# Multi-query attention with 16-wide heads: two heads share 32 rows of a query set, and two masked copies of the keys tell them apart

## The chip, the cores and the metric

The kernel runs on one core of one Trainium2 chip. The time is device microseconds of one execution; several executions are taken and the median is quoted. Two kernels are compared through runs taken in the same rounds on the same chip. A difference under 2% counts as "same".

Engine names as in the profile: PE is the tensor engine, ACT the scalar engine, DVE the vector engine, POOL the GpSimd engine, SP the queue that issues DMAs.

## The reference, cut to what matters

Two identical layers, each an attention block and a gated mixer block. Sequence 2048, model width 512, 32 heads of 16, one shared key and value head:

```python
q = (x @ wq).reshape(B, S, 32, 16).transpose(0, 2, 1, 3)
k = x @ wk                                   # one key head for all 32 query heads
v = x @ wv
p = softmax(einsum('bhqd,bkd->bhqk', q, k) * 16 ** -0.5)
o = einsum('bhqk,bkd->bhqd', p, v)           # then @ wo
# x = x + A(layernorm(x)); x = x + B(layernorm(x)); both twice
```

B is the mixer: gelu, a 2048 x 2048 mix over the sequence, and an output projection.

## The kernel before

The work of attention is 4096 *blocks*: 128 keys by 512 queries of one head, 2048 in each layer. A block is one matmul with 32 contracted rows, one exponential over 128 x 512, and one value matmul. Four heads sit at partitions 0, 32, 64 and 96 of a *query set* of 512 columns. A head has only 16 numbers per query, so 16 of each 32 rows are zeros that come out of zero-padded weights:

```python
# zero-padded query weights: 8 groups of 4 heads, each head 16 columns of weight and 16 of zero
wqv = self.wq_pad[:].rearrange("p kd hg (j r) -> p kd (hg j) r", r=32)[:, :, :, 0:DH]
c0 = rows(wqv[:, :, 0:8, :], wqn[:, :, 0:8, :], m, lq[0], 512, 1.2)                # ACT
c1 = rows(wqv[:, :, 8:32, :], wqn[:, :, 8:32, :], m, lq[1], 1536, 3.0, "pool")     # POOL
# ... cut: one query set = 4 heads x 512 columns: PE projects, DVE or ACT evicts
ins = e.matmul(self.b32(b)[:, i * n:(i + 1) * n], self.wq_pad[:, kd, g.hg + i, :],
               self.xnTA[:, g.t0 // 128:(g.t0 + n) // 128, kd, :], start=(kd == 0), stop=(kd == KD - 1))
# ... cut: the score matmul of one block
return e.matmul(self.b32(bank), self.kT[32 * j:32 * j + 32, kt * 128:(kt + 1) * 128],
                self.qs[32 * j:32 * j + 32, g.q.slot, :], tile_position=(32 * j, 0), start=True, stop=True)
```

ACT takes most blocks, two or three at a time. DVE takes the rest: it copies the scores out of PSUM with a multiply-add and runs a polynomial for the exponential, about 2.5 us a block.

This file does not write its instructions down; it *plans* them. At build time a list scheduler walks through all operations with assumed durations and latencies, decides for every engine which operation comes next, which engine evicts a bank (copies a result out of PSUM, where matmuls write), and which blocks go to DVE, and then writes out that fixed order:

```python
LAT = {"pe": 0.22, "act": 0.22, "dve": 0.14, "pool": 0.12, "sp": 0.0}   # assumed latency of a result, us
AHEAD = 1200.0   # more warm-up near the ends of a head group
WARM = 800.0     # warm-up: how many columns above 3060 per 3.41 us the planner keeps PE at
NQS = 6          # slots for query sets
# ... cut: the warm-up stream puts in a matmul on zeros whenever PE would fall below the limit
t = sc.below(f, TICK_COLS + WARM + (AHEAD if near else 0.0))
# ... cut: priority of a query set (small is early)
pr = 0.4 if g.ci == 0 and g.hg == 0 else 0.8 if g.hg < 2 else (2.2 if ... else 1.5)
```

The softmax here doesn't subtract the row's maximum and nothing guards it: scores larger than these inputs give would overflow.

Of the kernel before, what the change touches and what calls it, by code (L numbers as in the profile page):

```python
# [13 lines left out]
P = 128  # L14
# [361 lines left out]
AHEAD = 1200.0  # L376
# [3 lines left out]
WARM = 800.0  # L380
# [3 lines left out]
NQS = 6  # L384
# [9 lines left out]
def d_sb(n, rate):  # L394
    return n * rate + 0.066
# [14 lines left out]
class Group:  # L410

    __slots__ = ("layer", "ci", "hg", "nh", "t0", "n", "units", "q", "evac", "index")


class QSet:
    __slots__ = ("grp", "op", "slot", "left", "reads", "index")
# [10 lines left out]
class Kern:  # L427
    def __init__(self, nc, A_x, A_wq, A_wk, A_wv, A_wo, B_x, B_w_in, B_w_sp, B_b_sp, B_w_out, out):
# [27 lines left out]
        self.kT = sb([P, S], BF16, "kT")  # L456
        self.V = sb([P, self.NT, 128], BF16, "V")
        self.wq_pad = sb([P, KD, 8, 128], BF16, "wq_pad")
# [98 lines left out]
    def load(self, A_x, A_wq, A_wk, A_wv, A_wo, B_b_sp):  # L557
        sc = self.sc
        xs = A_x[0].rearrange("(t p) d -> p t d", p=P)
        wq_nat = self.z1s[:, 0:2048].rearrange("p (kd n) -> p kd n", kd=KD)  # L560
        wk_nat = self.z1s[:, 2048:2112].rearrange("p (kd n) -> p kd n", kd=KD)
        wv_nat = self.z1s[:, 2112:2176].rearrange("p (kd n) -> p kd n", kd=KD)
# [11 lines left out]
        def ld_q(c0, c1, eng):  # L574
            return self.dma(lambda e: e.dma_start(wq_nat[:, :, c0:c1], wq_d[:, :, c0:c1]), (), f"ldq{c0}", 1024 * (c1 - c0),
                            1.2 if eng == "act" else 5.0, eng)
# [31 lines left out]
        def vm(ap, n, prio):  # L608
            return sc.op("dve", lambda e: e.memset(ap, 0.0), d_sb(n, 0.26e-3), (), prio)

        def rows(dst, src, m, ld, n, prio, eng="act"):
            if eng == "act":
                return sc.op("act", lambda e: e.activation(dst, src, ACTF.Copy), d_act(n), [m, ld], prio)
            return sc.op("pool", lambda e: e.tensor_copy(dst, src), n * 1.0e-3 + 0.2, [m, ld], prio)
        m = vm(self.wk_rep[:], 512, 0.1)
        self.c_wk = rows(self.wk_rep[:].rearrange("p kd (g r) -> p kd g r", r=32)[:, :, :, 0:DH],
                         wk_nat[:, :, None, :].to_broadcast([P, KD, 4, DH]), m, lk, 256, 1.0)
# [3 lines left out]
        m = vm(self.wq_pad[:], 4096, 0.11)  # L621
        wqv = self.wq_pad[:].rearrange("p kd hg (j r) -> p kd (hg j) r", r=32)[:, :, :, 0:DH]
        wqn = wq_nat.rearrange("p kd (h r) -> p kd h r", r=DH)
        c0 = rows(wqv[:, :, 0:8, :], wqn[:, :, 0:8, :], m, lq[0], 512, 1.2)
        c1 = rows(wqv[:, :, 8:32, :], wqn[:, :, 8:32, :], m, lq[1], 1536, 3.0, "pool")
        self.c_wq = [c0, c0] + [c1] * 6
        m = vm(self.V[:], 2048, 0.13)
        self.z1s_free = [self.c_wk, self.c_wv, c0, c1]
# [55 lines left out]
    def layer_keys(self, layer):  # L684
        sc = self.sc
        for p in range(8):
            def build(p=p):
# [25 lines left out]
                def kcp(b):  # L713
                    return self.kT[:, p * 256:(p + 1) * 256], self.b32(b)[:, 0:256]

                def vcp(b):
# [3 lines left out]
                kc = dict(fn=lambda e, b: e.tensor_copy(*kcp(b)), dur=d_psum(256), prio=pr - 0.1, deps=kd_,  # L720
                          alts=[("act", lambda e, b: e.activation(*kcp(b), ACTF.Copy), d_act(256) + 0.1)])
                vc = dict(fn=lambda e, b: e.tensor_copy(*vcp(b)), dur=d_psum(128), prio=pr, deps=[self.c_v] + vd_,  # L722
                          alts=[("act", lambda e, b: e.activation(*vcp(b), ACTF.Copy), d_act(128) + 0.1)])
                if p < 2:
                    _, (k,) = sc.job([(kpe, 4 * d_mm(256))], [kc], evs + [self.c_wk], pr)
                    _, (v,) = sc.job([(vpe, 8 * d_mm(128))], [vc], evs + [self.c_wv], 0.9)
                else:
                    _, (k, v) = sc.job([((lambda e, b: (kpe(e, b), vpe(e, b))[1]), 4 * d_mm(256) + 8 * d_mm(128))], [kc, vc],
                                       evs + [self.c_wk, self.c_wv], pr)
                self.xnTA_ev[(layer, p)] = evs  # L730
                for t in ts:
                    self.k_op[(layer, t)] = k
# [10 lines left out]
    def layer_groups(self, layer):  # L743
        t0 = 0
        for ci, n in enumerate(self.chunks):
            nh = 512 // n
            for hg in range(0, 8, nh):
                g = Group()
                g.layer, g.ci, g.hg, g.nh, g.t0, g.n = layer, ci, hg, nh, t0, n
                g.index = len(self.groups)  # L750
                q = g.q = QSet()
                q.grp, q.op, q.left, q.reads = g, None, 4 * self.NT, []
                q.index = g.index
                q.slot = q.index % NQS
                self.qsets.append(q)
# [34 lines left out]
    def make_q(self, q, war=()):  # L790
# [4 lines left out]
        def pe(e, b, h):  # L795
            ins = None
            for i in range(g.nh):
# [961 lines left out]
```

## Time and profile before

| | before |
|---|---|
| median, 3 runs | 1837.04 us (1836.0 to 1838.01) |
| ACT, DVE, PE busy | 95%, 93%, 86% |
| first exponential starts | 18.1 us |
| from the last exponential of layer 1 to the first of layer 2 | 869.2 to 907.5 us |
| last exponential ends, execution ends | 1781.0, 1834.8 us |

The page's first lines, busy time by engine:

```profile
span 1834.8 us, 30175 instructions
## 1 busy us (share of the span) xinstructions
PE 1583.2 (86%) x11848; PEld 476.9 (26%) x11934; DVE 1704.0 (93%) x2917; ACT 1741.6 (95%) x1572; POOL 50.8 (3%) x90
```

The shares average over stages. The table by windows splits them: the first layer's exponentials, the first 100 us of the second layer, the rest of its exponentials, and the end. Columns: window, its length, busy us of PE, PEld, DVE, ACT and POOL, granted clock, DMA share, GB/s.

```profile
18.00:868.00 850.00, 733.07 (x5618) 213.33 (x5653) 792.70 (x1310) 844.71 (x737) 17.34 (x28) 1.00 0.16 41
907.00:1007.00 100.00, 82.59 (x611) 27.45 (x614) 87.74 (x170) 83.90 (x89) 5.76 (x12) 0.98 0.15 30
1007.00:1781.00 774.00, 670.55 (x5060) 189.22 (x5091) 728.51 (x1202) 770.49 (x668) 15.15 (x22) 1.00 0.08 23
1781.00:1835.00 54.00, 48.32 (x270) 22.79 (x273) 44.90 (x110) 19.19 (x38) 1.09 (x2) 1.00 0.31 95
```

In the first and third row ACT is busy for all but 5.3 and 3.5 us: it is the wall there, and nothing that PE or DVE saves counts unless it takes work or waiting from ACT. In the second row ACT idles 16 us; it waits for the second layer's keys, which follow the first layer's last mixer steps. In the fourth it has little to do.

The groups by form. Columns: line, engine, operation, tiles, shapes, count, then busy us and mean ns of one, then idle time before them and its releasers.

```profile
L1378 ACT ACTIVATE Pa<-ps_all 128x1536 bf16<-128x1536 f32 x716 | 1147.1, 1602 | 11.0 <-PE ps_all L1706 9.5
L1378 ACT ACTIVATE Pa<-ps_all 128x1024 bf16<-128x1024 f32 x715 | 843.3, 1179 | 1.0 <-PE ps_all L1706 0.8
...
L1562 DVE TENSOR_SCALAR E<-ps_all 128x512 f32<-128x512 f32 x516 | 351.2, 684 | 27.1 <-PE ps_all L1706 24.1
...
L1687 PE MATMUL ps_all<-zero 128*128 128x512 bf16 x846 | 269.1, 391 | 15.2 <-DVE st L1034 3.2 <-ACT z2n L1014 1.5 <-DVE gp L1133 1.5
...
L800 PE MATMUL ps_all<-xnTA,wq_pad 128*128 128x512 bf16 x192 | 54.4, 394 | 2.1 <-DVE V L722 0.9 <-DVE qs L809 0.8 <-DVE E L1562 0.2
...
L809 DVE CAST qs<-ps_all 128x512 bf16<-128x512 f32 x58 | 39.7, 684 | 4.0 <-PE ps_all L800 3.7
...
L721 ACT ACTIVATE kT<-ps_all 128x256 bf16<-128x256 f32 x16 | 6.8, 426 | 8.7 <-PE ps_all L708 5.5 <-PE ps_all L700 3.2
...
L810 ACT ACTIVATE qs<-ps_all 128x512 bf16<-128x512 f32 x6 | 3.6, 597 | 4.7 <-PE ps_all L800 4.7
```

Line 1562 counts the blocks that DVE takes: 516. Lines 809 and 810 are the 64 query evictions, line 721 the 16 key copies, line 800 the query projections (with smaller forms, 73.3 us of PE), line 1687 the warm-up matmuls.

The start, as ACT saw it; columns of the timeline are start, us, engine, line, operation, tiles, shapes, count, and in brackets the idle time before it:

```profile
12.61 0.60 ACT L678 ACTIVATE xnTA<-ps_all 128x512 bf16<-128x512 bf16 x1 [2.12 <-PE ps_all L670]
13.91 0.38 ACT L721 ACTIVATE kT<-ps_all 128x256 bf16<-128x256 f32 x1 [0.70 <-PE ps_all L700]
15.50 0.60 ACT L810 ACTIVATE qs<-ps_all 128x512 bf16<-128x512 f32 x1 [1.20 <-PE ps_all L800]
17.20 0.60 ACT L810 ACTIVATE qs<-ps_all 128x512 bf16<-128x512 f32 x1 [1.11 <-PE ps_all L800]
17.77 0.28 ACT L723 ACTIVATE V<-ps_all 128x128 bf16<-128x128 f32 x1
18.10 1.45 ACT L1378 ACTIVATE Pa<-ps_all 128x1536 bf16<-128x1536 f32 x1
```

Two query sets are evicted before the first exponential, though it needs one. Line 678 waits for PE's transpose of a tile `xn` that DVE makes in line 653. The POOL copy of the padded weights:

```profile
10.51 1.46 POOL L614 COPY wq_pad<-z1s 128x1536 bf16<-128x1536 bf16 x1
```

```profile
9.76 0.41 DVE L653 TENSOR_SCALAR xn<-X,mv,rs 128x512 bf16<-128x512 bf16 x1
...
10.76 1.37 DVE L653 TENSOR_SCALAR xn<-X,mv,rs 128x512 bf16<-128x512 bf16 x1
```

The same DVE instruction takes 0.41 us without that copy and 1.37 us while POOL copies the padded weights.

### The profile page before, as it was taken

To read this page: it belongs to the slowest core of one execution; us is meant where nothing else is said; L and a number is where in the kernel's file an instruction comes from. 1 tells how busy PE (TensorE), PEld (TensorE's weight loads), DVE (VectorE), ACT (ScalarE), POOL (GpSimd) and SP (SyncE) were. 2 spreads that over 40 slices of the span, in tenths; PEclk is the share of its full clock that TensorE was granted. 3 is DMA by queue.
4 is the path that set the end of the run, shared out by engine and by line. 5 is a ranking of instruction groups with operands and counts; after the bars stand their busy time and mean duration, and the time that the engine had idled before them with its cause. 6 is when DMAs were issued, how large, how long until landed. Compare 5 with 4: busy or idle time off the path is not lost.

```text
span 1834.8 us, 30175 instructions
## 1 busy us (share of the span) xinstructions
PE 1583.2 (86%) x11848; PEld 476.9 (26%) x11934; DVE 1704.0 (93%) x2917; ACT 1741.6 (95%) x1572; POOL 50.8 (3%) x90
## 2 busy tenths in 40 slices
PE   8888898888889889898888788887888899999898
PEld 3222222222222222232432222222222222222234
DVE  8999999999999999976879999999999999998778
ACT  7999999999999999999569999999999999999983
POOL 2000000000000000000100000000000000000000
PEclk9999999999999999999999999999999999999999
DMA  9800010000010010111120000100000100103023
GB/s 260 218 1 1 7 41 1 1 1 18 7 41 24 24 47 29 39 58 56 52 50 1 1 1 9 38 1 1 1 18 7 41 24 24 47 21 96 9 56 111
DMA packets 122965, 68.04 MB, mean 37 GB/s; under 512 B 76997, under 2 KB 119241, under 8 KB 122825
## 3 DMA queue, kind: packets, MB, share of 16 engines
q1 hardware_dynamic: 121240, 65.95, 13.3%
q8 instruction: 95, 1.56, 0.3%
q10 hardware_dynamic: 1584, 0.16, 0.1%
q14 instruction: 46, 0.37, 0.1%
HBM read 30.97 MB, written 17.83 MB: 27 GB/s over the span
## 4 chain that ended last, share of the span: by engine, by line
ACT 43%; PE 21%; issue 18%; DVE 17%; DMA 0%; POOL 0%; ACTq 0%; POOLq 0%
ACT Pa L1378 41%; PE ps_all L1120 5%; PE ps_all L1706 5%; PE ps_all L1454 3%; DVE E L1562 3%; PE ps_all L1212 2%; DVE Pd L1593 2%; DVE E L1591 1%; DVE E L1587 1%; DVE E L1589 1%; PE ps_all L1687 1%; DVE st L638 1%; DVE z2n L954 1%; PE ps_all L800 1%; DVE E L1590 1%
## 5 line engine op out<-in xcount | busy, mean ns | idle before, releaser
L1378 ACT ACTIVATE Pa<-ps_all 128x1536 bf16<-128x1536 f32 (+1 forms) x1433 | 1627.7, 1390 | 12.0 <-PE ps_all L1706 10.3
L1706 PE MATMUL ps_all<-qs,kT 32*128 32x512 bf16 x4096 | 566.2, 386 | 202.7 <-ACT Pa L1378 187.8
L1562 DVE TENSOR_SCALAR E<-ps_all 128x512 f32<-128x512 f32 x516 | 351.2, 684 | 27.1 <-PE ps_all L1706 24.1
L1706 PEld LDWEIGHTS ps_all<-qs,kT 32*128 32x128 bf16 x4096 | 139.3, 91 | 758.1 <-ACT Pa L1378 710.3
L1454 PE MATMUL ps_all<-Pa,V 128*32 128x512 bf16 x3580 | 322.8, 386 | 0.0
L1593 DVE SCALAR_TENSOR_TENSOR Pd<-E 128x1024 uint16<-128x1024 f32 x260 | 314.6, 1210 | 4.4
L1687 PE MATMUL ps_all<-zero 128*128 128x512 bf16 x846 | 269.1, 391 | 15.2 <-DVE st L1034 3.2
L1120 PE MATMUL ps_all<-wsT,z2n 128*128 128x512 bf16 x655 | 186.6, 382 | 7.1 <-issue 3.5
L1454 PE MATMUL ps_all<-Pd,V 128*32 128x512 bf16 x516 | 182.3, 385 | 0.0
L1589 DVE TENSOR_TENSOR E<-E 128x1024 f16<-128x1024 f16 x260 | 176.9, 680 | 4.9
L1591 DVE TENSOR_TENSOR E<-E 128x1024 f16<-128x1024 f16 x260 | 177.1, 681 | 4.2
L1587 DVE TENSOR_SCALAR E<-E 128x1024 f16<-128x1024 uint16 x260 | 176.6, 679 | 1.5
L1590 DVE TENSOR_SCALAR E<-E 128x1024 f16<-128x1024 f16 x260 | 107.5, 413 | 1.9
L1687 PEld LDWEIGHTS ps_all<-zero 128*128 128x128 bf16 x846 | 62.9, 98 | 150.6 <-issue 98.6
L1133 DVE TENSOR_TENSOR gp<-ps_all,gp 128x512 f16<-128x512 f32 x112 | 75.5, 684 | 24.1 <-PE ps_all L1120 23.8
L1454 PEld LDWEIGHTS ps_all<-Pa,V 128*32 128x32 bf16 x3580 | 64.5, 94 | 121.5 <-issue 118.5
L1120 PEld LDWEIGHTS ps_all<-wsT,z2n 128*128 128x128 bf16 x714 | 53.7, 97 | 99.3 <-issue 58.5
L800 PE MATMUL ps_all<-xnTA,wq_pad 128*128 128x512 bf16 (+2 forms) x384 | 73.3, 316 | 2.2 <-DVE V L722 0.9
L943 PE MATMUL ps_all<-w_in_r,xnTB 128*128 128x448 bf16 x256 | 63.5, 356 | 2.0 <-DVE E L1562 0.7
L979 PE MATMUL ps_all<-xnTB,w_in_r 128*128 128x512 bf16 (+2 forms) x336 | 62.4, 310 | 1.0 <-DVE gp L990 0.2
L1212 PE MATMUL ps_all<-E 128*128 128x512 bf16 x213 | 52.0, 380 | 4.2 <-DVE E L1197 2.0
L642 POOL TENSOR_SCALAR ve<-mv 128x2 f32<-128x2 f32 (+1 forms) x28 | 9.2, 330 | 1383.9 <-DVE mv L640 1383.7
(88 smaller groups left out, 1002.6 us busy)
## 6 DMA issues: line engine op xcount, KB each, us to landing
wsT_scratch<-gp SPq DMA_DIRECT2D x16, 512.0 KB, 3.6
wsT<-wsT_scratch SPq DMA_DIRECT2D x8, 1024.0 KB, 5.2
z1s<-z_scratch SPq DMA_DIRECT2D x16, 448.0 KB, 3.8
wsT<-wsT_scratch SPq DMA_DIRECT2D x8, 512.0 KB, 3.6
z_scratch<-z1s SPq DMA_DIRECT2D x4, 896.0 KB, 5.2
X<-in_A_x_dram SPq DMA_DIRECT2D x8, 256.0 KB, 5.5
out_dram<-X SPq DMA_DIRECT2D x16, 128.0 KB, 1.9
w_in_r<-in_B_w_in_dram SPq DMA_DIRECT2D x1, 1792.0 KB, 10.0
```

The source lines that it names most:

```text
L800: ins = e.matmul(self.b32(b)[:, i * n:(i + 1) * n], self.wq_pad[:, kd, g.hg + i, :], self.xnTA[:, g.t0 // 128:(g.t0 + n) // 128, kd, :], s ...
L1120: ins = e.matmul(self.b32(b), self.z2n[:, s, f * 128:(f + 1) * 128], w_[:, s - s0, :] if s - s0 < na or not spare else wsp[:, s - s0 - na, :],
L1378: return e.activation(k.Pa[:, base:base + n, :], k.b32(b0, n).rearrange("p (k q) -> p k q", k=n), ACTF.Exp, scale=SCALE)
L1454: ins = e.matmul(k.b32(k.pvb)[32 * j:32 * j + 32, :], k.V[:, u.kt, 32 * j:32 * j + 32], b.slot, tile_position=(0, 32 * j), start=u.first, ...
L1562: c = k.sc.op("dve", lambda e: e.tensor_scalar(k.ey[:, s, 512 * i:512 * (i + 1)], k.b32(j.bank.idx)[:, 0:512], E_LOG2, E_BIAS, op0=ALU.mul ...
L1587: o2 = sc.op("dve", lambda e: e.tensor_scalar(x, lo, E_X * 2.0 ** -16, E_X * E_A, op0=ALU.mult, op1=ALU.add), d_sb(n, 0.521e-3), self.ops ...
L1589: o3 = sc.op("dve", lambda e: e.tensor_tensor(w, x, x, ALU.mult), d_sb(n, 0.521e-3), [o2, self.wfree], pr)
L1590: o4 = sc.op("dve", lambda e: e.tensor_scalar(w, w, E_C, None, op0=ALU.add), d_sb(n, 0.26e-3), [o3], pr)
L1591: o5 = sc.op("dve", lambda e: e.tensor_tensor(w, w, x, ALU.mult), d_sb(n, 0.521e-3), [o4], pr)
L1593: o7 = sc.op("dve", lambda e: e.scalar_tensor_tensor(po.bitcast(U16), y, E_D, w, op0=ALU.add, op1=ALU.add), d_sb(n, 1.042e-3), [o5] + self ...
L1687: return e.matmul(k.b32(k.pvb if b is None else b.idx), k.zero[:], k.zero[:, None, :].to_broadcast([P, 4, P]), start=b is not None, stop=b ...
L1706: return e.matmul(self.b32(bank), self.kT[32 * j:32 * j + 32, kt * 128:(kt + 1) * 128], self.qs[32 * j:32 * j + 32, g.q.slot, :], tile_pos ...
```

## The change

The 16 zero rows are given to a second head. A query set now carries eight heads, and the plain weight needs no padding: columns 128 s to 128 s + 127 are eight whole heads. To keep the two heads of 32 rows apart there are two copies of the keys, one with the lower 16 rows of each 32 zero, one with the upper. So 64 query sets become 32 and 16 key copies become 32. Score matmuls, exponentials and value matmuls stay as they are. Two constants of the warm-up and the number of slots were set anew as well. The core of the diff, cuts marked:

```diff
-AHEAD = 1200.0
+AHEAD = 0.0
-WARM = 800.0
+WARM = 1200.0
-NQS = 6
+NQS = 4
 ... (cut)
-        self.kT = sb([P, S], BF16, "kT")
+        self.kT = sb([P, 2, S], BF16, "kT")
+        self.mask = sb([P, 2], FP32, "mask")
-        self.wq_pad = sb([P, KD, 8, 128], BF16, "wq_pad")
+        self.wq_r = sb([P, KD, D], BF16, "wq_r")
 ... (cut: the memset and the two padding copies go; wq is loaded straight into wq_r)
-                kc = dict(fn=lambda e, b: e.tensor_copy(*kcp(b)), dur=d_psum(256), prio=pr - 0.1, deps=kd_,
-                          alts=[("act", lambda e, b: e.activation(*kcp(b), ACTF.Copy), d_act(256) + 0.1)])
+                ks = [dict(fn=lambda e, b, v=v: e.tensor_scalar(*kcp(b, v), self.mask[:, v:v + 1], None, op0=ALU.mult),
+                           dur=d_psum(256), prio=pr - 0.1 + 0.2 * v, deps=kd_ + [self.c_mask[v]],
+                           alts=[("act", lambda e, b, v=v: e.activation(*kcp(b, v), ACTF.Copy, scale=self.mask[:, v:v + 1]),
+                                  d_act(256) + 0.1)]) for v in range(2)]
 ... (cut: groups come in pairs v = 0, 1 that share a query set)
-                        ins = e.matmul(self.b32(b)[:, i * n:(i + 1) * n], self.wq_pad[:, kd, g.hg + i, :],
+                        ins = e.matmul(self.b32(b)[:, i * n:(i + 1) * n], self.wq_r[:, kd, 128 * (q.s0 + i):128 * (q.s0 + i + 1)],
 ... (cut)
-        pr = 0.4 if g.ci == 0 and g.hg == 0 else 0.8 if g.hg < 2 else (2.2 if g.layer == 1 and g.ci == 0 and g.hg < NQS else 1.5)
+        pr = (0.4 if g.ci == 0 else 0.8) if q.s0 == 0 else (2.2 if g.layer == 1 and g.ci == 0 and q.s0 < NQS - 1 else 1.5)
 ... (cut)
-    return e.matmul(self.b32(bank), self.kT[32 * j:32 * j + 32, kt * 128:(kt + 1) * 128],
+    return e.matmul(self.b32(bank), self.kT[32 * j:32 * j + 32, g.v, kt * 128:(kt + 1) * 128],
```

More of the change, by code (lines that the diff above doesn't have):

```diff
@@ L410 @@
 class Group:
-    __slots__ = ("layer", "ci", "hg", "nh", "t0", "n", "units", "q", "evac", "index")
+    __slots__ = ("layer", "ci", "v", "t0", "n", "units", "q", "evac", "index")
 class QSet:
-    __slots__ = ("grp", "op", "slot", "left", "reads", "index")
+    __slots__ = ("grp", "s0", "ns", "op", "slot", "left", "reads", "index")
 class Unit:
@@ L559, in load @@
         xs = A_x[0].rearrange("(t p) d -> p t d", p=P)
-        wq_nat = self.z1s[:, 0:2048].rearrange("p (kd n) -> p kd n", kd=KD)
-        wk_nat = self.z1s[:, 2048:2112].rearrange("p (kd n) -> p kd n", kd=KD)
-        wv_nat = self.z1s[:, 2112:2176].rearrange("p (kd n) -> p kd n", kd=KD)
+        wk_nat = self.z1s[:, 0:64].rearrange("p (kd n) -> p kd n", kd=KD)
+        wv_nat = self.z1s[:, 64:128].rearrange("p (kd n) -> p kd n", kd=KD)
         def ld_x(p):
@@ L574, in ld_q @@
         def ld_q(c0, c1, eng):
-            return self.dma(lambda e: e.dma_start(wq_nat[:, :, c0:c1], wq_d[:, :, c0:c1]), (), f"ldq{c0}", 1024 * (c1 - c0),
+            return self.dma(lambda e: e.dma_start(self.wq_r[:, :, c0:c1], wq_d[:, :, c0:c1]), (), f"ldq{c0}", 1024 * (c1 - c0),
                             1.2 if eng == "act" else 5.0, eng)
@@ L607, in load, with vm @@
         self.c_mh = pm(self.mhalf[:], -0.5, 1, 0.3)
-        def vm(ap, n, prio):
-            return sc.op("dve", lambda e: e.memset(ap, 0.0), d_sb(n, 0.26e-3), (), prio)
+        def vm(ap, n, prio, val=0.0, deps=()):
+            return sc.op("dve", lambda e: e.memset(ap, val), d_sb(n, 0.26e-3), deps, prio)
         def rows(dst, src, m, ld, n, prio, eng="act"):
@@ L614, in rows @@
             return sc.op("pool", lambda e: e.tensor_copy(dst, src), n * 1.0e-3 + 0.2, [m, ld], prio)
-        m = vm(self.wk_rep[:], 512, 0.1)
-        self.c_wk = rows(self.wk_rep[:].rearrange("p kd (g r) -> p kd g r", r=32)[:, :, :, 0:DH],
-                         wk_nat[:, :, None, :].to_broadcast([P, KD, 4, DH]), m, lk, 256, 1.0)
+        m = vm(self.mask[:, 0:1], 1, 0.05)
+        for j in range(4):
+            m = vm(self.mask[32 * j:32 * j + DH, 0:1], 1, 0.05, 1.0, [m])
+        self.c_mask = [m, sc.op("dve", lambda e: e.tensor_scalar(self.mask[:, 1:2], self.mask[:, 0:1], -1.0, 1.0, op0=ALU.mult,
+                                                                 op1=ALU.add), 0.07, [m], 0.06)]
+        self.c_wk = rows(self.wk_rep[:].rearrange("p kd (g r) -> p kd g r", r=DH),
+                         wk_nat[:, :, None, :].to_broadcast([P, KD, 8, DH]), None, lk, 512, 1.0)
         m = vm(self.wv_rep[:], 512, 0.12)
@@ L620, in load @@
                          wv_nat[:, :, None, :].to_broadcast([P, KD, 4, DH]), m, lv, 256, 1.1)
-        m = vm(self.wq_pad[:], 4096, 0.11)
-        wqv = self.wq_pad[:].rearrange("p kd hg (j r) -> p kd (hg j) r", r=32)[:, :, :, 0:DH]
-        wqn = wq_nat.rearrange("p kd (h r) -> p kd h r", r=DH)
-        c0 = rows(wqv[:, :, 0:8, :], wqn[:, :, 0:8, :], m, lq[0], 512, 1.2)
-        c1 = rows(wqv[:, :, 8:32, :], wqn[:, :, 8:32, :], m, lq[1], 1536, 3.0, "pool")
-        self.c_wq = [c0, c0] + [c1] * 6
+        self.c_wq = [lq[0]] + [lq[1]] * 3
         m = vm(self.V[:], 2048, 0.13)
-        self.z1s_free = [self.c_wk, self.c_wv, c0, c1]
+        self.z1s_free = [self.c_wk, self.c_wv]
         self.c_v = pm(self.V[:].rearrange("p t (c r) -> p t c r", r=32)[:, :, :, DH], 1.0, 64, 0.8, [m])
@@ L711, in vpe, with kcp @@
                     return ins
-                def kcp(b):
-                    return self.kT[:, p * 256:(p + 1) * 256], self.b32(b)[:, 0:256]
+                def kcp(b, v):
+                    return self.kT[:, v, p * 256:(p + 1) * 256], self.b32(b)[:, 0:256]
                 def vcp(b):
@@ L724, in build @@
                 if p < 2:
-                    _, (k,) = sc.job([(kpe, 4 * d_mm(256))], [kc], evs + [self.c_wk], pr)
+                    _, k = sc.job([(kpe, 4 * d_mm(256))], ks, evs + [self.c_wk], pr)
                     _, (v,) = sc.job([(vpe, 8 * d_mm(128))], [vc], evs + [self.c_wv], 0.9)
                 else:
-                    _, (k, v) = sc.job([((lambda e, b: (kpe(e, b), vpe(e, b))[1]), 4 * d_mm(256) + 8 * d_mm(128))], [kc, vc],
-                                       evs + [self.c_wk, self.c_wv], pr)
+                    _, (k0, v, k1) = sc.job([((lambda e, b: (kpe(e, b), vpe(e, b))[1]), 4 * d_mm(256) + 8 * d_mm(128))],
+                                            [ks[0], vc, ks[1]], evs + [self.c_wk, self.c_wv], pr)
+                    k = [k0, k1]
                 self.xnTA_ev[(layer, p)] = evs
                 for t in ts:
-                    self.k_op[(layer, t)] = k
+                    self.k_op[(layer, 0, t)], self.k_op[(layer, 1, t)] = k
                     self.v_op[(layer, t)] = v
@@ L745, in layer_groups @@
         for ci, n in enumerate(self.chunks):
-            nh = 512 // n
-            for hg in range(0, 8, nh):
+            ns = 512 // n
+            for s0, v in [(s, v) for s in range(0, 4, ns) for v in range(2)]:
                 g = Group()
-                g.layer, g.ci, g.hg, g.nh, g.t0, g.n = layer, ci, hg, nh, t0, n
+                g.layer, g.ci, g.v, g.t0, g.n = layer, ci, v, t0, n
                 g.index = len(self.groups)
-                q = g.q = QSet()
-                q.grp, q.op, q.left, q.reads = g, None, 4 * self.NT, []
-                q.index = g.index
-                q.slot = q.index % NQS
-                self.qsets.append(q)
+                if v == 0:
+                    q = QSet()
+                    q.grp, q.s0, q.ns, q.op, q.left, q.reads = g, s0, ns, None, 8 * self.NT, []
+                    q.index = len(self.qsets)
+                    q.slot = q.index % NQS
+                    self.qsets.append(q)
+                g.q = q
                 g.units = []
@@ L796, in pe @@
             ins = None
-            for i in range(g.nh):
-                for kd in ((0, 1), (2, 3))[h] if g.nh == 1 else range(4):
-                    if g.nh == 1 or i // (g.nh // 2) == h:
-                        ins = e.matmul(self.b32(b)[:, i * n:(i + 1) * n], self.wq_pad[:, kd, g.hg + i, :],
+            for i in range(q.ns):
+                for kd in ((0, 1), (2, 3))[h] if q.ns == 1 else range(4):
+                    if q.ns == 1 or i // (q.ns // 2) == h:
+                        ins = e.matmul(self.b32(b)[:, i * n:(i + 1) * n], self.wq_r[:, kd, 128 * (q.s0 + i):128 * (q.s0 + i + 1)],
                                        self.xnTA[:, g.t0 // 128:(g.t0 + n) // 128, kd, :], start=(kd == 0), stop=(kd == KD - 1))
@@ L806, in make_q @@
         pairs = range(g.t0 // 256, (g.t0 + n - 1) // 256 + 1)
-        pr = 0.4 if g.ci == 0 and g.hg == 0 else 0.8 if g.hg < 2 else (2.2 if g.layer == 1 and g.ci == 0 and g.hg < NQS else 1.5)
-        pe_last, (op,) = sc.job([((lambda e, b: pe(e, b, 0)), 2 * g.nh * d_mm(n)), ((lambda e, b: pe(e, b, 1)), 2 * g.nh * d_mm(n))],
+        pr = (0.4 if g.ci == 0 else 0.8) if q.s0 == 0 else (2.2 if g.layer == 1 and g.ci == 0 and q.s0 < NQS - 1 else 1.5)
+        pe_last, (op,) = sc.job([((lambda e, b: pe(e, b, 0)), 2 * q.ns * d_mm(n)), ((lambda e, b: pe(e, b, 1)), 2 * q.ns * d_mm(n))],
                                 [dict(fn=lambda e, b: e.tensor_copy(*cp(b)), dur=d_psum(512), prio=pr, deps=list(war),
                                       alts=[("act", lambda e, b: e.activation(*cp(b), ACTF.Copy), d_act(512) + 0.1)])],
-                                [x for p in pairs for x in self.xnTA_ev[(g.layer, p)]] + self.c_wq[g.hg:g.hg + g.nh], pr)
+                                [x for p in pairs for x in self.xnTA_ev[(g.layer, p)]] + self.c_wq[q.s0:q.s0 + q.ns], pr)
         q.op = op
@@ L839, in nm @@
             if g.n == 128:
-                out = self.on[:, 0, g.hg * 64:(g.hg + 4) * 64].rearrange("p (i j d) -> p i j d", j=4, d=DH)
+                out = self.on[:, 0, :].rearrange("p (i j v d) -> p i j v d", j=4, v=2, d=DH)[:, :, :, g.v, :]
                 s0, s1 = 0, 4
             else:
-                hg = g.hg + h
-                out = self.on[:, 0:nq, hg * 64:(hg + 1) * 64].rearrange("p i (j d) -> p i j d", d=DH)
+                c = 128 * (g.q.s0 + h)
+                out = self.on[:, 0:nq, c:c + 128].rearrange("p i (j v d) -> p i j v d", j=4, v=2)[:, :, :, g.v, :]
                 s0, s1 = h * nq, (h + 1) * nq
@@ L858, in finish_group @@
         self.norms.append(m)
-        if g.hg + g.nh == 8:
+        if g.v == 1 and g.q.s0 + g.q.ns == 4:
             norms = self.norms
@@ L1287, in peek @@
             deps.append(g.q.op)
-            o = k.k_op.get((g.layer, b.unit.kt))
+            o = k.k_op.get((g.layer, g.v, b.unit.kt))
             if o is None or o.start is None:
@@ L1495, in deps @@
         g = x.unit.grp
-        return [g.q.op, k.k_op[(g.layer, x.unit.kt)]]
+        return [g.q.op, k.k_op[(g.layer, g.v, x.unit.kt)]]
     def take(self, t, js):
@@ L1535, in take @@
                 return None
-            o = k.k_op.get((layer, un.kt))
+            o = k.k_op.get((layer, un.grp.v, un.kt))
             if o is None or o.start is None or o.vis > t:
```

## The prediction

> **What bounds the kernel now.** The page gives ScalarE (ACT) 95%, VectorE (DVE) 93%, PE 86% of 1834.8 us. By 50-us windows, from 50 to about 840 us and from 1000 to about 1740 us ACT is busy 49 to 50 of every 50 us, nearly all of it the exponentials of line 1378; DVE mostly 47 to 49.5, PE 40 to 47. In the groups by form, line 1378 is busy 1627.7 us for 3580 score blocks, 0.455 us of ACT each; the other 516 blocks go through DVE's polynomial (lines 1562, 1587 to 1593: 1304 us, 2.53 us of DVE each). So ACT is the wall, and DVE relieves it at 5.6 us for 1. ACT idles about 93 us in all: the start (first exponential at 18.1 us), the change of layers (869 to about 965 us) and the closing mixer (from about 1780 us), where PE, DVE and latency lead.
>
> **What the change does.**
> 1. Query projections halve: 64 sets become 32. Line 800 costs PE 73.3 us; 36.7 us go. But warm-up matmuls (line 1687, 846, 269 us, 13 us of a window in mid-layer) are issued whenever the stream falls below a column limit and refill this; WARM up from 800 to 1200 adds more. PE stays at 85 to 90%. PE is not the wall, so this is worth almost nothing outside the start and the change of layers.
> 2. Query evictions halve: 64 of 512 columns, 58 on DVE at 0.684 us. About 20 us of DVE and 1 to 2 us of ACT go.
> 3. Key copies double, 16 more. A masked copy from PSUM should cost what a plain one does: the Trainium skill, "VectorE: DVE Perf Modes", section "Why PSUM operands drop a tier", holds fp32 PSUM operands to the 1x mode; the trace agrees, cast and multiply-add of 128x512 both take 0.68 us. 16 x 0.38 = +6 us, most on DVE.
> 4. The padded weights go: a 1.77-us DVE memset, a 0.63-us ACT copy and a 1.46-us POOL copy in the first 12 us. The first query set serves eight heads, so the second (4 matmuls, 0.4 us each) no longer goes ahead of the first scores.
> 5. Score and value matmuls and exponentials stay.
>
> **What it is worth.** Net DVE saving about 16 us. If DVE turns it into blocks, both engines stay full and the span falls by 16 x 0.455/(2.53+0.455) = 2.4 us, 5 more blocks on DVE. ACT savings, about 1 us, count nearly whole. Start: 2 us. Change of layers: one query set before the first scores, fewer evictions: 1.5 us. Clock: five windows after the start show 0.97; the skill's "TensorE: Matmul & The Clock Gate", Part 1, gives a window of about 3.4 us at half or full rate, and 0.03 x 50 us agrees with one half-rate interval. ACT loses about 0.7 us in such a window; the higher WARM may recover 2 us. Freer banks and PE in the dense mixer windows: 1 to 2 us. Sum about 11 us.
>
> **Prediction: 1826 us, 1813 to 1836; faster by over 2% 0.04, within 2% 0.94, slower by over 2% 0.02.**
>
> **What would show it.** Line 800 about 37 us; query evictions 32; key copies 32 at about 0.38 us; warm-up matmuls over 950; DVE blocks 520 to 535; ACT full mid-layer; first exponential at 15.5 to 17 us; fewer 0.97 windows.
>
> **What would make it wrong.** Extra warm-up matmuls delaying scores so that ACT waits; the chained second key copy holding banks in the change of layers (slower); a reshuffled order that lets DVE take many more blocks (faster).

## The result, and the profile after

| | before | after |
|---|---|---|
| median of 4 runs each | 1836.52 us (1835.57 to 1838.01) | 1832.13 us (1832.09 to 1835.02) |
| ratio | 1 | 0.9979 (95% interval 0.9962 to 0.9997) |
| span of the profiled run | 1834.8 us | 1830.0 us |

A ratio is the mean time of one kernel's runs over that of the other's of the same rounds, so it is not quite the ratio of the medians quoted. The change made the kernel about 4 us faster. I had forecast 11.

The lines that answer to those of before, page, windows, groups:

```profile
span 1830.0 us, 30222 instructions
## 1 busy us (share of the span) xinstructions
PE 1597.4 (87%) x11863; PEld 480.3 (26%) x11947; DVE 1697.1 (93%) x2924; ACT 1739.0 (95%) x1565; POOL 49.1 (3%) x89
```

```profile
14.00:863.00 849.00, 740.81 (x5621) 212.95 (x5654) 794.50 (x1322) 843.62 (x734) 19.87 (x30) 1.00 0.16 43
901.00:1001.00 100.00, 84.32 (x618) 27.66 (x619) 89.58 (x180) 82.42 (x84) 5.86 (x12) 0.98 0.14 30
1001.00:1775.00 774.00, 678.63 (x5071) 193.78 (x5103) 724.14 (x1192) 768.60 (x664) 13.62 (x22) 0.99 0.09 23
1775.00:1830.00 55.00, 49.75 (x276) 23.02 (x279) 44.67 (x110) 20.41 (x41) 1.10 (x2) 1.00 0.31 93
```

```profile
L1382 ACT ACTIVATE Pa<-ps_all 128x1536 bf16<-128x1536 f32 x714 | 1147.3, 1607 | 11.2 <-PE ps_all L1710 9.7
L1382 ACT ACTIVATE Pa<-ps_all 128x1024 bf16<-128x1024 f32 x716 | 846.7, 1183 | 1.6 <-PE ps_all L1710 1.5
...
L1566 DVE TENSOR_SCALAR E<-ps_all 128x512 f32<-128x512 f32 x522 | 355.1, 683 | 26.5 <-PE ps_all L1710 22.8
L1691 PE MATMUL ps_all<-zero 128*128 128x512 bf16 x1051 | 327.5, 392 | 17.4 <-ACT z1s L1014 3.2 <-DVE E L1566 2.1 <-DVE E L1593 1.8
...
L804 PE MATMUL ps_all<-xnTA,wq_r 128*128 128x512 bf16 x96 | 25.5, 381 | 1.1 <-DVE qs L813 0.5 <-DVE gp L994 0.3 <-DVE E L1566 0.3
...
L813 DVE CAST qs<-ps_all 128x512 bf16<-128x512 f32 x30 | 20.4, 679 | 0.1
...
L721 ACT ACTIVATE kT<-ps_all,mask 128x256 bf16<-128x256 f32 x16 | 7.6, 478 | 14.1 <-PE ps_all L707 11.0 <-PE ps_all L699 3.0
L719 DVE TENSOR_SCALAR kT<-ps_all,mask 128x256 bf16<-128x256 f32 x16 | 7.6, 478 | 1.7 <-ACT V L724 1.6
...
L814 ACT ACTIVATE qs<-ps_all 128x512 bf16<-128x512 f32 x2 | 1.2, 592 | 0.0
```

The counts changed as forecast: 32 evictions instead of 64, 32 key copies (at 0.478 us each and not 0.38), 1051 warm-up matmuls that more than refill PE, 522 blocks on DVE instead of 516. Yet ACT's idle time did not fall: in the second row it is 17.6 us where it was 16.1, and in the third 5.4 where it was 3.5. The start:

```profile
11.21 0.60 ACT L677 ACTIVATE xnTA<-ps_all 128x512 bf16<-128x512 bf16 x1 [0.38 <-PE ps_all L669]
12.51 0.98 ACT L721 ACTIVATE kT<-ps_all,mask 128x256 bf16<-128x256 f32 x2 [0.70 <-PE ps_all L699]
13.39 0.59 ACT L814 ACTIVATE qs<-ps_all 128x512 bf16<-128x512 f32 x1
13.87 0.28 ACT L724 ACTIVATE V<-ps_all 128x128 bf16<-128x128 f32 x1
14.60 2.37 ACT L1382 ACTIVATE Pa<-ps_all 128x1536 bf16<-128x1536 f32 x2 [0.46 <-PE ps_all L1710]
```

The first exponential comes 3.5 us earlier. The matching tile of DVE's layer norm now takes 0.40 us instead of 1.37:

```profile
10.32 0.40 DVE L652 TENSOR_SCALAR xn<-X,mv,rs 128x512 bf16<-128x512 bf16 x1
```

Part of the 3.5 us is chance. In the profiled run of before the clock stood at half rate from 13.9 us for 3.4 us, just over the eight query matmuls; in that of after it did not. Profiles of re-drawn plans of before (below) without such a stretch have their first exponential at 16.4 us.

Splitting the two spans at the first and last exponential of each layer gives the ledger of this pair, from the two traces. Positive is time gained, in us:

| part | before | after | gained |
|---|---|---|---|
| start, up to the first exponential | 18.1 | 14.6 | 3.5 |
| first layer's exponentials, first to last | 851.1 | 848.8 | 2.3 |
| change of layers, last to first | 38.3 | 38.4 | -0.1 |
| second layer's exponentials | 873.5 | 873.2 | 0.3 |
| end, after the last exponential | 53.8 | 55.0 | -1.1 |

The sum is 4.8 us. So the whole net gain is reached at 863 us; the second layer gives nothing and the end gives some back. The question for the experiments was where the other 6 us went.

### The profile page after: what moved, and what is told of

The parts are those of the page before. It is cut to its first block, busy times and chain, and to the rows that moved or that the text cites. A ratio compares the mean times of both kernels' runs of the same rounds, so it can differ in the third digit from the quotient of the medians. Undisturbed runs are those within 1.5% of the kernel's fastest.

```text
span 1830.0 us, 30222 instructions
## 1 busy us (share of the span) xinstructions
PE 1597.4 (87%) x11863; PEld 480.3 (26%) x11947; DVE 1697.1 (93%) x2924; ACT 1739.0 (95%) x1565; POOL 49.1 (3%) x89
## 4 chain that ended last, share of the span: by engine, by line
ACT 43%; PE 21%; DVE 18%; issue 17%; POOL 1%; DMA 0%; ACTq 0%; POOLq 0%
ACT Pa L1382 41%; PE ps_all L1710 6%; PE ps_all L1124 6%; PE ps_all L1458 4%; DVE E L1566 3%; DVE Pd L1597 2%; PE ps_all L1216 2%; DVE E L1595 1%; DVE E L1593 1%; DVE E L1591 1%; DVE st L637 1%; PE ps_all L1691 1%; PE ps_all L915 1%; DVE E L1594 1%; DVE gp L1137 1%
## 5 line engine op out<-in xcount | busy, mean ns | idle before, releaser
L1566 DVE TENSOR_SCALAR E<-ps_all 128x512 f32<-128x512 f32 x522 | 355.1, 683 | 26.5 <-PE ps_all L1710 22.8
L1691 PE MATMUL ps_all<-zero 128*128 128x512 bf16 x1051 | 327.5, 392 | 17.4 <-ACT z1s L1014 3.2
L1597 DVE SCALAR_TENSOR_TENSOR Pd<-E 128x1024 uint16<-128x1024 f32 (+1 forms) x262 | 317.8, 1213 | 4.1
L1593 DVE TENSOR_TENSOR E<-E 128x1024 f16<-128x1024 f16 (+1 forms) x262 | 178.9, 683 | 5.2
L1595 DVE TENSOR_TENSOR E<-E 128x1024 f16<-128x1024 f16 (+1 forms) x262 | 178.3, 681 | 3.7
L1591 DVE TENSOR_SCALAR E<-E 128x1024 f16<-128x1024 uint16 (+1 forms) x262 | 178.4, 681 | 1.3
L1691 PEld LDWEIGHTS ps_all<-zero 128*128 128x128 bf16 x1051 | 79.8, 98 | 186.6 <-issue 128.0
L1594 DVE TENSOR_SCALAR E<-E 128x1024 f16<-128x1024 f16 (+1 forms) x262 | 108.8, 415 | 1.8
L1195 ACT ACTIVATE E<-ps_all 128x512 f16<-128x512 f32 (+1 forms) x52 | 24.6, 551 | 24.0 <-PE ps_all L1183 24.0
L826 DVE CAST oT<-ps_all 128x512 bf16<-128x512 f32 x64 | 43.7, 683 | 3.1 <-PE ps_all L1458 2.7
```

What stands on the lines that cost most here:

```text
L1566: c = k.sc.op("dve", lambda e: e.tensor_scalar(k.ey[:, s, 512 * i:512 * (i + 1)], k.b32(j.bank.idx)[:, 0:512], E_LOG2, E_BIAS, op0=ALU.mul ...
L1591: o2 = sc.op("dve", lambda e: e.tensor_scalar(x, lo, E_X * 2.0 ** -16, E_X * E_A, op0=ALU.mult, op1=ALU.add), d_sb(n, 0.521e-3), self.ops ...
L1593: o3 = sc.op("dve", lambda e: e.tensor_tensor(w, x, x, ALU.mult), d_sb(n, 0.521e-3), [o2, self.wfree], pr)
L1594: o4 = sc.op("dve", lambda e: e.tensor_scalar(w, w, E_C, None, op0=ALU.add), d_sb(n, 0.26e-3), [o3], pr)
L1595: o5 = sc.op("dve", lambda e: e.tensor_tensor(w, w, x, ALU.mult), d_sb(n, 0.521e-3), [o4], pr)
L1597: o7 = sc.op("dve", lambda e: e.scalar_tensor_tensor(po.bitcast(U16), y, E_D, w, op0=ALU.add, op1=ALU.add), d_sb(n, 1.042e-3), [o5] + self ...
```

## The experiments

My first theory: the gain is the start plus what DVE's freed time is worth, and the two new constants are neutral. Rivals: the constants earn or cost something; query sets cost more than DVE's time because they hold PE and PSUM banks; the gain is mostly an accident of the planned order.

### The constants and the start

**a_oldwarm**, the kernel after with the old constants:

```diff
-AHEAD = 0.0
+AHEAD = 1200.0
-WARM = 1200.0
+WARM = 800.0
```

> The kernel after, with the two warm-up constants of before (AHEAD 1200, WARM 800). My theory, that ScalarE is the wall and the constants are not part of the gain: 1832 us within 1.5, ratio 0.997 to 0.9985, about 850 warm-up matmuls instead of 1051, first exponential still at 14 to 15 us. Rival 1, the constants earn part of the gain (they keep the clock up in the start): 1834 to 1837 us. Rival 2, the constants cost something (more warm-up matmuls in front of scores): 1827 to 1830 us, with less idle ScalarE in the second layer.

Measured: 1832.4 us, ratio 0.9980 (0.9968 to 0.9993), 931 warm-up matmuls where I had expected about 850, first exponential at 14.8 us. The constants of after are worth nothing that can be seen here.

**b_newwarm**, the kernel before with the new constants:

```diff
-AHEAD = 1200.0
+AHEAD = 0.0
-WARM = 800.0
+WARM = 1200.0
```

> The kernel before, with the two warm-up constants of after. My theory: within 1.5 us of before (1835 to 1838), over 1000 warm-up matmuls, the number of half-rate stretches not clearly lower. Rival 1, the constants earn: 1832 to 1835 us, with the half-rate stretch at 14 us gone. Rival 2, they cost: 1838 to 1841 us.

Measured: 1840.3 us, 1.0029 (1.0016 to 1.0041), with 979 warm-up matmuls. Its profiled run has one half-rate stretch (6.8 us) in place of six, and is no faster for it. The edit that changes nothing in after costs 5 us in before. My expectation, within 1.5 us of before, was missed; neither "they earn" nor "they cost" fits both runs.

**b_q2late**, the kernel before with one priority changed:

```diff
-        pr = 0.4 if g.ci == 0 and g.hg == 0 else 0.8 if g.hg < 2 else (
+        pr = 0.4 if g.ci == 0 and g.hg == 0 else 0.8 if g.hg < 1 else (
```

> The kernel before, with only the priority of the second query set lowered, so that it no longer goes ahead of the first scores. No set is shared, no weight changed. If the start's gain of 3.5 us is the second set (0.9 us at full clock, 1.7 us at half): first exponential at 16 to 17.2 us and 1835 to 1836 us in all. If it is the memset, the padding copies and the clock: first exponential within 0.5 us of 18.1.

Measured: 1845.6 us, 1.0055 (1.0043 to 1.0068): 10 us *slower*. In the trace the start behaves as foreseen, though less so: first exponential at 17.7 us, with the half-rate stretch again over the query matmuls. The loss lies elsewhere: the first layer's exponentials take 856.5 us instead of 851.1 and the second's 879.6 instead of 873.5. No operation is added or removed there. But the rule holds for the second set of each of the three 512-column chunks of queries in both layers, so six sets got a lower priority, and this run is not a pure change of order elsewhere. A missed expectation, and the first hint.

**a_dupq**, the kernel after with 30 of its 32 query sets projected and evicted a second time, into a tile nobody reads:

```diff
+        if g.ci > 0 or q.s0 > 0:
+            dpe, (self.qd_last,) = sc.job([ ...the same matmuls... ],
+                                          [dict(fn=lambda e, b: e.tensor_copy(self.qd[:], self.b32(b)[:, 0:512]), ...)], ..., pr)
+            for p in pairs:
+                self.xnTA_read[p].append(dpe)
```

> The kernel after, with every query set but the first of each layer's first chunk projected and evicted a second time into a spare tile: 62 evictions, PE line again near 72 us, still no padding and the same start. It is the price of 30 query sets by themselves. My theory (DVE time is worth 0.15 us of span per us): 30 x 0.684 x 0.15 = 3.1 us, so 1834 to 1837 us, 5 to 7 fewer blocks on DVE. Rival, that query sets hold PE and banks and so cost more: 1838 us or more. Rival, that they cost nothing because the order of the schedule decides: 1831 to 1833 us.

Measured: 1830.75 us, 0.9971 (0.9958 to 0.9985). With 20 us more DVE work it is not slower than after. Read alone, this says that the sets which the change removes cost nothing. Its trace disagrees with that reading. The groups by form of this kernel:

```profile
L1576 DVE TENSOR_SCALAR E<-ps_all 128x512 f32<-128x512 f32 x508 | 345.8, 684 | 30.0 <-PE ps_all L1720 27.4
...
L816 DVE CAST qd<-ps_all 128x512 bf16<-128x512 f32 x28 | 19.2, 686 | 2.3 <-PE ps_all L806 2.1
L823 DVE CAST qs<-ps_all 128x512 bf16<-128x512 f32 x28 | 19.1, 683 | 2.9 <-PE ps_all L806 2.7
```

The added evictions (qd) took 19.2 us of DVE, and DVE took 508 blocks where after took 522, so ACT did more. But in the second layer ACT idled 16.8 us where after idled 22.5. This looks like a real cost covered by a luckier order. So I turned to measuring the order itself.

### Re-drawing the plan

The edit is one assumed latency in the planner, which changes no operation, only the order: 0.14 us becomes 0.141, 0.143 or 0.139.

```diff
-LAT = {"pe": 0.22, "act": 0.22, "dve": 0.14, "pool": 0.12, "sp": 0.0}
+LAT = {"pe": 0.22, "act": 0.22, "dve": 0.141, "pool": 0.12, "sp": 0.0}
```

**b_null1** and **a_null1** (0.141):

> The kernel before with one number of its build-time planner moved by 1 ns (the assumed latency of a VectorE result, 140 to 141 ns). Same work, instruction for instruction of the same kinds; only the order it plans differs. Theory order: a plan re-drawn like this moves the time by 2 to 6 us either way, mostly up, since the constants of before were picked for its own plan: 1834 to 1844 us. Rival, the order does not matter and the 4 us of the change come from the work it removes: 1835 to 1837.5 us.

> The kernel after with the same 1 ns. Theory order: anywhere from 1827 to 1838 us, with the start at 14.6 us unchanged and the differences in the first 75 us of the second layer and between 500 and 870 us of each layer. Rival: 1831 to 1833 us.

**b_null2** and **a_null2** (0.143):

> The kernel before with the same number moved by 3 ns. Theory order: 1834 to 1844 us, and not the same as with 1 ns. Rival: 1835 to 1837.5 us.

> The kernel after with the same 3 ns. Theory order: 1827 to 1838 us. Rival: 1831 to 1833 us. If the change has a worth of its own, as in my prediction, the mean over the re-drawn plans of after should lie 5 us or more under that of before; if its gain was the draw, the means coincide.

**b_null3** and **a_null3** (0.139):

> The kernel before, planner's latency moved by 1 ns the other way (139 ns). So far: before itself 1.0000, its two re-drawn plans 1.0008 and 1.0057. Theory, before holds a favourable plan: this one lands above it again, 1838 to 1850 us. Rival, the plans of before scatter evenly about 1836.5: 1832 to 1837 us as likely as not.

> The kernel after, 139 ns. So far 0.9979, 0.9948, 0.9983. Theory: 1828 to 1836 us, so that the mean of four plans of after is about 0.5% under that of four plans of before.

**dupq_null1** and **dupq_null2**, the doubled query sets with 0.141 and 0.143:

> The kernel after with each query set but two made and evicted twice, plan re-drawn with 141 ns. The first such run, 1830.75 us, seemed to say that 30 query sets cost nothing, but in its trace DVE took 508 blocks instead of 515 to 525 and the exponentials took 5 us more of ScalarE. Theory, the sets have a price of 3 to 8 us and that run was a lucky plan: 1833 to 1842 us. Rival, the sets are free: 1827 to 1834 us, the range of after.

> The same with 143 ns. Theory: 1833 to 1842 us, DVE blocks again near 508, so that the mean of the three doubled runs lies above the mean of after. Rival: 1827 to 1834 us.

**dupq_null3** (0.139):

> The kernel after with doubled query sets, plan re-drawn with 139 ns. So far 0.9971, 0.9997, 1.0022 of before, against 0.9948 to 0.9984 for four plans of after. Theory, a price of 3 to 6 us: 1833 to 1840 us. Rival, no price: 1828 to 1833 us.

Measured, as ratio to before and median:

| assumed latency | before | after | after, sets doubled |
|---|---|---|---|
| 0.140 (as given) | 1 (1836.5) | 0.9979 (1832.1) | 0.9971 (1830.8) |
| 0.141 | 1.0008 (1839.0) | 0.9948 (1828.4), again 0.9962 (1829.1) | 0.9997 (1835.2) |
| 0.143 | 1.0057 (1848.4) | 0.9983 (1834.4) | 1.0022 (1840.7) |
| 0.139 | 1.0063 (1848.0) | 0.9984 (1833.0) | 1.0008 (1838.8) |
| mean of four plans | 1.0032 | 0.9975 | 1.0000 |

(The two takes of 0.141 of after are averaged first. The 95% intervals of single ratios are about 0.0013 to 0.002 either way; that of dupq_null3 is 0.9987 to 1.003.)

Three things follow.

First, moving an assumed latency by 1 ns moved the kernel before by 0.63%, 12 us. That is more than the effect under study.

Second, before as given is the best of its four plans (with 0.141 it is a tie, 0.9991 to 1.0025), and the two other small edits of before, b_newwarm and b_q2late, came out slower too. Its order is a favourable one. That its constants were picked for that is likely but not shown.

Third, on the mean of four plans the change is worth 0.0057, 10.4 us, with a standard error of about 0.0018 (3 us) worked out from the scatter of the plans. The doubled sets lie 0.0024, 4.5 us, above after, with a standard error of 0.0013; so their price is probable from the times, and the traces make it firm, as follows.

For each kernel the profiled runs of the four plans give, between the first and last exponential of the layers, how long ACT worked and how long it idled:

| means of four profiled plans, us | before | after | sets doubled |
|---|---|---|---|
| blocks taken by DVE | 517 (515 to 520) | 521 (517 to 525) | 510 (508 to 513) |
| ACT at exponentials | 1627.0 | 1624.8 | 1629.1 |
| ACT at other work | 72.8 | 70.7 | 73.0 |
| ACT idle | 29.5 (24.8 to 34.2) | 27.1 (26.3 to 28.2) | 26.0 (21.3 to 30.6) |

ACT's work hardly depends on the plan. Exponentials and other work together are 1701 to 1703 us in each of the four doubled plans and 1692 to 1698 us in each of the four of after: the 30 sets cost 6.5 us of ACT work on average, and the two do not overlap. Idle time is what the plan draws: 24.8 us in before as given, 33.4 and 34.2 in its two slow draws.

Where a draw loses is plain in b_null3. First the window of the first 100 us of its second layer, then ACT's timeline in it:

```profile
903.00:1003.00 100.00, 81.75 (x577) 28.48 (x579) 78.34 (x159) 75.71 (x83) 5.89 (x12) 0.98 0.14 30
```

```profile
946.24 3.36 ACT L1378 ACTIVATE Pa<-ps_all 128x1024 bf16<-128x1024 f32 x3 [0.35 <-PE ps_all L1706]
958.34 0.38 ACT L721 ACTIVATE kT<-ps_all 128x256 bf16<-128x256 f32 x1 [8.73 <-PE ps_all L708]
```

ACT is busy 75.7 us of the 100 where it was 83.9 in before. It runs out of keys once, for 8.7 us. In this plan the last of the 16 residual additions of the first layer (line 1217) starts 49.6 us after the second layer's first exponential, in before 40.2 us; each key tile needs the layer norm of such a tile, so the last key copy comes at 57.9 us instead of 48.5. The same kernel work in another order reaches ACT later.

### Best against best, and the second key copy

**b_best** and **a_best**: the plan that the kernel's own planner rates best in a search, 120 latencies for before (0.1235, own constants), 160 combinations of latency and constants for after (0.1344, WARM 800, AHEAD 0). The planner's ratings only chose the plans; they are no measurements.

```diff
-"dve": 0.14
+"dve": 0.1235      # b_best; 0.1344 and WARM = 800.0 in a_best
```

> The kernel before with the plan that its own planner rates best among 120 values of the same latency (123.5 ns). If before already held about the best plan it can get, 1832 to 1837 us, within 0.3% of before. If re-drawing has much room left for it, under 1830 us, and the change would then be worth nothing beyond its plan.

Measured: 1836.6 us, 0.9999 (0.9981 to 1.0017). Before already held about as good a plan as this search finds.

> The kernel after with the plan rated best in a search of the same size over latency and the two warm-up constants (134.4 ns, WARM 800, AHEAD 0). Theory, the change is worth 3 to 8 us at best against best: 1826 to 1830 us, and 3 us or more under b_best. Rival: the same as b_best within 2 us.

Measured: 1834.75 us, 0.9985 (0.9959 to 1.0011), six runs from 1828.7 to 1841.7 us, on a chip where before itself went from 1833.2 to 1845.1. This settles nothing.

**a_null1_again** and **a_best2**: the first is a_null1 unchanged; the second is after with 0.1421 and its own WARM and AHEAD:

```diff
-"dve": 0.14
+"dve": 0.1421
```

> The kernel after with 141 ns, as a_null1, in five rounds on another occasion. If its 0.9948 was the plan: 0.994 to 0.9965 of before again, and under 0.9979, the ratio of after. If it was that chip: 0.997 to 0.999.

> The kernel after with 142.1 ns and its own WARM 1200 and AHEAD 0, rated by its planner as high as a_best and a_null1. If the planner's rating is a guide and WARM 1200 keeps the runs together: 0.994 to 0.997 of before, with runs within 4 us of each other. If the rating is no guide: 0.997 to 0.999.

Measured: 1829.1 us, 0.9962 (0.9950 to 0.9975), five runs within 1.4 us; and 1828.9 us, 0.9963 (0.9949 to 0.9976), five runs within 2.7 us. Both are clearly under before, by about 7 us, and their medians are 3 us under that of after, though the intervals of the ratios overlap with that of after. Best against best, through before: 0.9963 over 0.9999, 0.36%, 6.6 us. Whether the scatter of a_best comes from its lower WARM or from that chip stays open, since before scattered there as well. The scatter goes with the clock: the granted clock was 0.983 and 0.984 in the runs of 1840.4 and 1841.7 us, 0.995 and 0.996 in those of 1829.8 and 1828.7.

**a_onekey**, the kernel after with the second key copy left out and the first used for both head sets; its result is wrong:

```diff
-                                  d_act(256) + 0.1)]) for v in range(2)]
+                                  d_act(256) + 0.1)]) for v in range(1)]
-    ... self.kT[32 * j:32 * j + 32, g.v, ...
+    ... self.kT[32 * j:32 * j + 32, 0, ...
```

> The kernel after with one key copy for both head sets: the 16 second copies are gone, and the result is wrong on purpose. If the second copies cost what I predicted (6 us of DVE, so 1 us of span) this cannot be told from the scatter of plans: 1827 to 1835 us. If they hold up the change of layers, 1823 to 1828 us with idle ScalarE in the second layer under 16 us.

Measured: 1833.8 us, 0.9987 (0.9960 to 1.0015), a single plan. ACT idled 16.2 us in the second layer, and that layer's exponentials were the shortest of all runs, 865.4 us, but the end took 59.9 us instead of 54. The median lies inside the scatter of the plans of after (1828.4 to 1834.4 us), so no price of the second copies can be told from it.

## Why the prediction was wrong, and where it was right

Against the ledger of the two given kernels, and against the means of four plans each (profiled spans, us gained):

| term of the prediction | forecast | this pair | means of four plans |
|---|---|---|---|
| start | 2 | 3.5 | 2.3 |
| ACT work: fewer blocks (2.4), fewer evictions (1) | 3.4 | 5.2 | 4.3 |
| ACT idle within the layers: clock (2), banks and dense windows (1 to 2) | 3.5 | -2.7 | 2.5 |
| change of layers | 1.5 | -0.1 | 0.0 |
| the end | 0 | -1.1 | 1.8 |
| sum | about 11 | 4.8 | 10.9 |

- **What bounds the kernel: right.** ACT stays full through both layers. PE lost 38 us of query projections and 205 more warm-up matmuls took their place; the span did not notice.
- **DVE's freed time: right, somewhat small.** I forecast 2.4 us and 5 more blocks from 16 us of DVE, and 1 us of ACT. The pair shows 6 more blocks; the means show 3.5 more, 2.2 us less of exponentials and 2.1 us less of other ACT work. Doubling 30 sets cost 10.5 blocks and 6.5 us of ACT work, so a query set is dearer than my formula says, 0.2 us each: DVE gave up 10.5 x 2.53 = 27 us of blocks for some 19 us of evictions. The runs do not show whether PE, the bank or the order leaves the rest of that time empty.
- **Key copies: the count right, the size wrong.** I took 0.38 us from the plain ACT copy. A masked one takes 0.478 us on ACT and on DVE. The Trainium skill, "ScalarE: Activation LUTs", section "What ACT_TABLE_LOAD costs", says that each operand of one value per partition adds about 93 ns; ACT's median copy went from 383 to 474 ns, which agrees. I had not looked it up. Half of the copies went to ACT, where I had put most on DVE. The 1x rate of fp32 PSUM operands, from "VectorE: DVE Perf Modes", section "Why PSUM operands drop a tier", is not contradicted: no masked copy on DVE (466 to 484 ns in after) was faster than a plain one (413 to 426 ns, the seven that other plans of before put on DVE).
- **Start: right in size, wrong in part.** 2.3 us on the mean, 3.5 in the pair with its half-rate stretch. I credited mainly the second query set (4 matmuls of 0.4 us). In the traces the second set accounts for about 0.4 us (b_q2late against before, b_null1 against after, counted from the end of the last xnTA copy before the first exponential), and that copy ends 1.3 to 1.6 us earlier (13.2 us in all four plans of before, 11.6 to 11.9 in those of after), before any query matmul. With the 1.7 us lost in the half-rate stretch these make up the 3.5 us of the pair. That 2 us was near the mean is thus partly luck. The slow DVE instruction beside the POOL copy fits the earlier copy: in all seven profiled kernels with padded weights it took 1.37 to 1.47 us and ended 0.15 us after POOL's copy did, whether it had started 0.14 or 0.24 us into it, and in those without padding it took 0.4 us. The Trainium skill, "GPSIMD Engine Reference", section "1. Specifications", lists POOL's SBUF interfaces as shared with VectorE. No run here removes that copy alone, so this is a reading of the traces and not a tested cause.
- **Clock: the price of a stretch about right, the recovery wrong.** I credited 2 us to a higher WARM. Both profiled runs have five half-rate stretches after the start, where I had forecast fewer. Each lasts 3.4 us, as the skill's "TensorE: Matmul & The Clock Gate", Part 1, says of its window. Between plans the stretches followed neither the warm-up matmuls nor the time: the profiled run of a_null2 had none and spanned 1831.4 us, that of a_best2 had six and spanned 1828.1. Within one plan the time does go with the granted clock, which they lower: over the 125 executions of the experiments, each compared with the mean of its kernel in its batch, the time rises by 1.04 us for each 0.001 that the granted clock falls (correlation -0.90). One stretch lowers the clock of the whole span by 0.0009, so it costs about 1 us by this estimate; I had put 0.7. What failed is that more warm-up matmuls would remove stretches: the granted clock was 0.994 in the profiled run of before and 0.995 in that of after. (The doubled plans ran at 0.9976 on average and the four of after at 0.9958, so at equal clock the 30 sets would cost about 6 us by the same slope, an estimate near their 6.5 us of ACT work.)
- **Change of layers: wrong.** 38.3 us in the mean of both kernels. What ends it is the chain of mixer, layer norm and keys; the query set is on it by 0.5 us: from the start of the last key matmuls before it to the first exponential it took 3.2 us in before, with two sets, and 2.7 us in after and in b_q2late, with one. The chain before that took as much longer in after.

**The step that failed** is "Sum about 11 us", which counts on 3.5 us less idle time of ACT within the layers; in this pair it grew by 2.7 us. The sum is near what the change is worth, 10.4 us by the mean ratios with a standard error of 3 us, but not what these two files differ by; and that it is so near is partly luck, since the 1.5 us at the change of layers did not come, and the 1.8 us at the end, which I had not forecast, come from one slow plan (b_null2, 61.2 us against 53.8 to 54.7). The terms that I mis-sized are the clock, the banks and dense windows, and the change of layers, together 5 us in the sum and -2.8 us in this pair, with -1.1 us at the end on top. What the runs showed in their place is a term I left out. The order of before is a favourable draw: 24.8 us of ACT idle where four plans average 29.5. Changing anything draws again, and after drew an ordinary plan, 27.5 us where its four average 27.1. My list of what would make the prediction wrong did name a reshuffled order, but only as a chance of a gain, without a size. The range, 1813 to 1836, did hold the result; its centre was too low by about what the favourable order of before saves in idle time, 29.5 - 24.8 = 4.7 us.

Not settled: what makes one plan's idle time larger than another's, beyond the late keys seen in b_null3 and b_null2; the price of the second key copies; whether a lower WARM lowers the clock of some runs, as in a_best, or that chip did; and the number of slots, which went from 6 sets of four heads to 4 of eight and which no run varies alone. The means of idle time, 29.5 and 27.1 us, are closer than the plans of before among themselves, so the 2.5 us in the last column are not shown to belong to the change.

The version to keep is the kernel after with the planner's latency at 141 or 142.1 ns: 1829 us.

## What to carry to other kernels

When a program's order comes from a planner, a change is compared through several plans of each side, not one: here 1 ns in an assumed latency moved the time by up to 0.6%, and a single ablation (a_dupq) said that 30 query sets are free when four plans say 4.5 us. A tuned kernel is a selected draw, so expect to give back part of any gain until the new version has had as many draws. And look for the quantity that the draw leaves alone: the work of the wall engine told the doubled sets from after without overlap, while its idle time carried the noise.

## What the Trainium skill lacked or had wrong

- "TensorE: Matmul & The Clock Gate", Part 1: its window agrees (every half-rate stretch within the profiled spans lasts 3.4 us, or two or three times that), but I found no limit in it that tells when a stretch comes in a kernel whose PE is busy 86% of the time. Here profiled runs had 0 to 6 of them with no relation to the warm-up matmuls: none with 1065, six with 1041, three with 848.
- "VectorE: DVE Perf Modes": I found no cost for an operand of one value per partition. A DVE copy of 128x256 keys from PSUM to bf16 took 413 to 426 ns plain (seven, in b_null2, b_null3, b_q2late and b_best) and 476 ns with the mask (median of 16 in after).
- No page that I read warns that a fixed instruction order, re-drawn without changing any operation, moves a kernel's time: 1836.5 to 1848.4 us for four plans of before, 1828.4 to 1834.4 us for four of after.
